# Strassen output block in PSUM: the first product is copied into the second one's bank, and the second accumulates on it

## Chip, cores and metric

The kernel runs on one core of one Trainium2 chip. The metric is the device time of one execution in microseconds (us). It was measured at 535.56 us, the median of 3 runs (535.33 to 535.83).

Engines are named as the profile names them: PE is the matrix engine (PEld its weight loads), DVE the vector engine, ACT the scalar engine, POOL GpSimd, SP the engine whose queue issues the DMAs.

## The reference

A gated linear attention recurrence (4 batches, 8 heads, 768 steps, head size 48) gives 3072 tokens of 384 features. A two-layer network with a hard-swish in the middle follows. Cut to what matters here:

```python
# attention: state = alpha[t] * state + k[t] v[t]^T;  y[t] = q[t] @ state
x = attn_out.transpose(0, 2, 1, 3).reshape(B * S, H * D)   # (3072, 384)
h = x @ w_in                                               # (3072, 2048)
g = h * np.clip(h + 3.0, 0.0, 6.0) / 6.0
return (g @ w_out).astype(np.float32)                      # (3072, 384)
```

Everything is fp32. The change lies in the last product, `g @ w_out`.

## The kernel before

**Tiling.** Tokens are worked off in 24 chunks of 128 (index j) for the attention and in 12 groups of 256 (index g, two chunks) for the network. While the network of group g runs, the attention of later chunks runs between its steps. For groups 2 to 11 the first layer is a fast matrix product of 20 block products (`product1`); for groups 1 to 11 the second layer is a Strassen-like product of 7 block products (`product`). Groups 0 and 1 have other first layers, and group 0 has a plain second one.

**Order.** Nothing reorders the work: `run` (from line 751) walks through a long string of words such as `P.5.0.0` under a manual schedule, and each word issues the instructions of one step. Each engine runs its own instructions in the order of the words; semaphores hold an instruction until what it reads is written and what it overwrites has been read. An instruction that waits holds everything behind it on its engine.

**The words** that this document speaks of (g is the group):

- `M.g.i[.m]`, PE, line 600: block product i of layer 1, four matmuls 128x128x128 into a whole PSUM bank of 512 columns. With m it opens bank m (there are four, `bank_m[0..3]`, line 470), without m it goes on accumulating in the bank of product i-1.
- `n.g.i.z`, ACT, line 606: copies the bank's running sum after product i to SBUF. The next product of the same bank overwrites that sum, so it waits for `n`.
- `o.g.o.step`, DVE, line 610: adds kept sums; with the last step it reads a PSUM bank, and that frees it. `e.g.o`, ACT, lines 619 and 494, and `h.g.o`, DVE, lines 623 and 498: the hard-swish of output block o. Blocks 0 and 1 make the quarter a11 of the hidden tile, 2 and 3 make a12, 4 and 5 a21, 6 and 7 a22.
- `s.g.i`, DVE, line 658: sums of quarters for layer 2.
- `P.g.i[.m]`, PE, line 685: product i of layer 2, eight matmuls into the first 192 columns of a bank, each recorded as two passes (16 records). Products 0, 2, 4 and 6 accumulate one after the other in one bank (`x_t`), 3 and 5 in a second one (`y_t`), and product 1, which is a12 times a block of the weights, has a bank of its own (`z_t`). Product 1's first four matmuls need `h.g.2`, its last four `h.g.3`.
- `K.g.i`, ACT, lines 706 and 680: keeps a running sum in SBUF: K.g.0 the sum after product 0 (tile `p1`), K.g.1 the one after product 2 (`u2`), K.g.2 the one after product 3 (`p5`). Product 2 overwrites what K.g.0 reads, product 4 overwrites what K.g.1 reads, and so they wait for these copies.
- `G.g.i.z`, line 713: the output blocks into the SBUF tile `ohs[z]`. G.g.0 is product 1 (PSUM) plus `p1` (SBUF), one addition on DVE (line 719), and so are G.g.1 and G.g.2 with other sums; G.g.3 is a copy on ACT (line 716). `O.g.i` stores the block through SP's queue (line 724).
- `xc` (sums of x on DVE), `tk`, `ca`, `q`, `qa`, `sc`, `u`, `ya`, `yb`, `cy`, `sv`: steps of the attention and of the inputs that stand between.

The output block of words `K.g.0` and `G.g.0` before:

```python
name, after = [("p1", 0), ("u2", 2), ("p5", 3)][i]        # K: nc.scalar.copy PSUM -> SBUF
kept(g, name, at_t[g, after])
...
after, other = [(1, "p1"), (4, "p5"), (5, "u2")][i]       # G.g.0, G.g.1, G.g.2
nc.vector.tensor_tensor(out=o, in0=at_t[g, after], in1=part_t.pop((g, other)), op=ALU.add)
```

Of the kernel before, what the change touches and what calls it, by code (L numbers as in the profile page):

```python
# [17 lines left out]
def kernel(  # L18
# [32 lines left out]
    nc = tc.nc  # L51
# [633 lines left out]
    def product(g, i, m=None):  # L685
# [6 lines left out]
            (lambda: whole(a12), b[1, 0], z_t, True, True),  # L692
# [13 lines left out]
    def keep2(g, i):  # L706
        name, after = [("p1", 0), ("u2", 2), ("p5", 3)][i]
        kept(g, name, at_t[g, after])
# [4 lines left out]
    def output2(g, i, z):  # L713
        o = oh_t[g, i] = ohs[z]
        if i == 3:
            nc.scalar.copy(out=o, in_=at_t[g, 6])
        else:
            after, other = [(1, "p1"), (4, "p5"), (5, "u2")][i]
            nc.vector.tensor_tensor(out=o, in0=at_t[g, after], in1=part_t.pop((g, other)), op=ALU.add)
# [30 lines left out]
    with tc.manual_schedule():  # L750
# [3 lines left out]
               dx.0 w.2 d2.2 kb.1.0 ck.1 lq.1 r.2 sm.0.1 st.1 tq.1.2 q.1 d3.2 z.0.3 d1.2 dx.2 lv.1.1  # L754
               u.1.3.1 sv.1.0 sm.1.0 p.2 sm.1.1 sc.1.0.2 m.1 ya.0.3 yb.0 cy.0 lq.2 w.1 d1.1 tq.2.1
               q.2 d4.2 lk.2 tk.2.3 k.2 fa.2.0 d4.0 st.2 sc.2.0.2 d2.1 d3.1 m.2 dx.1 d4.1 qa.1.1
               lk.3 la.3 ta.3.1 ca.3 la.4 fa.0.1 sv.1.1 w.3 r.3 ta.4.3 ca.4 r.4 tk.3.1 k.3 kb.2.0
               qa.1.0 d2.3 ya.1.2 yb.1 cy.1 fa.1.2 lq.3 ck.2 d1.3 p.3 d3.3 lv.2.2 u.2.3.2 sm.2.0
               d4.3 fb.2 tq.3.1 q.3 fb.1 qa.2.0 sm.2.1 sv.2.0 st.3 fr.0.2.0 fg.0.2 lk.4 tk.4.0
               sv.2.1 w.5 d2.5 k.4 d3.5 d1.5 qa.3.0 d4.5 qa.2.1 sc.3.1.3 m.3 w.6 d2.6 d1.6 d3.6 d4.6  # L760
               lv.3.0 lq.4 w.7 kb.3.2 fb.0 f.0.3.3 kb.4.0 ya.2.1 ck.3 u.3.3.2 sm.3.0 fr.0.3.1 fg.0.3
               fr.0.1.0 fg.0.1 qa.3.1 sv.3.0 sm.3.1 p.4 d2.7 sv.3.1 d1.7 d3.7 d4.7 f.0.5.0 fr.0.5.1
               fr.0.0.0 fg.0.5 fg.0.0 tq.4.3 ck.4 la.5 ta.5.2 f.0.6.3 ca.5 w.4 d2.4 ya.3.0 yb.3 cy.3
               fr.0.6.1 yb.2 cy.2 w.9 d2.9 q.4 qa.4.1 d1.4 d1.9 dx.4 la.6 w.8 d3.4 r.5 lk.5 w.10
               d3.9 p.5 ca.6 fg.0.6 d4.9 w.12 lq.5 lv.4.1 d2.8 d3.8 f.0.7.2 d1.8 st.4 d4.8 d4.4 w.11
               fr.0.7.0 fg.0.7 f.1.7.0 fr.1.7.1 fg.1.7 sc.4.0.2 m.4 f.1.1.1 fr.1.1.0 fg.1.1 f.1.3.3
               fr.1.3.1 d2.10 d1.10 tk.5.3 f.1.0.2 d2.12 d3.10 d4.10 w.13 fg.1.3 fr.1.0.0 fg.1.0 k.5
               d3.12 lq.6 f.1.6.0 f.1.2.1 u.4.1.0 sm.4.0 d1.12 d4.12 sv.4.0 qa.4.0 ya.4.2 fr.1.6.1
               fg.1.6 w.15 tq.5.3 fa.4.3 sv.4.1 d2.11 kb.5.1 d2.13 fr.1.2.0 f.1.4.2 fr.1.4.1 d1.11
               sm.4.1 q.5 r.6 d3.11 d3.13 fg.1.4 d4.11 lv.5.0 lk.6 tq.6 p.6 d2.15 d3.15 fg.1.2 d1.13  # L770
               d4.13 sc.5.0.3 yb.4 f.1.5.0 fr.1.5.1 fg.1.5 tk.6 m.5 b.1.0.2 fb.4 b.1.1 d1.15 d4.15
               st.5 y.5 w.14 la.7 lk.7 cy.4 d2.14 qa.5.1 ck.5 b.0.0.1 fr.0.4.0 d3.14 k.6 q.6 ca.7
               fg.0.4 d1.14 d4.14 x.0 y.1 y.10 b.0.1 y.0 y.2 u.5.2 P.1.0.0 K.1.0 qa.5.0 sv.5.0
               qa.6.1 P.1.1.3 b.0.2 b.1.2 kb.6.0 ya.5.3 y.6 s.1.0.0 sm.5.0 sv.5.1 G.1.0.0 tk.7
               s.1.1.1 s.1.2.3 x.1 yb.5 cy.5 b.1.3 sc.6.1.2 lv.6.2 ck.6 u.6.3.0 s.1.3.2 x.2 P.1.2
               b.0.3 K.1.1 y.7 s.1.4 s.1.5 y.11 y.3 r.7 xc.2.1 x.3 y.4 y.8 xc.2.3 k.7 xc.2.0 xc.2.4
               y.9 y.12 y.16 y.13 y.15 P.1.3.3 K.1.2 P.1.4 bo.1 P.1.5 xc.2.5 G.1.1.1 P.1.6 y.14 y.17
               y.19 xc.2.6 sm.6.0 G.1.2.2 y.20 M.2.0.2 lv.12.1 la.8 O.1.1 O.1.0 ca.8 y.18 y.21 y.23
               so.1 G.1.3.3 n.2.0.8 bo.0 lq.7 lv.7.0 O.1.2 m.6 xc.2.2 xc.2.10 xc.2.7 tq.7 r.8 p.7
               xc.2.8 sv.6.1 M.2.15.3 M.2.1 kb.7.3 n.2.1.9 M.2.16 M.2.2 n.2.2.10 M.2.7.0 n.2.7.11  # L780
               sm.6.1 xc.2.9 q.7 p.8 M.2.3 M.2.4 n.2.4.12 M.2.8 o.2.0.0 M.2.5 n.2.5.13 qa.7.0 sv.6.0
               st.7 lk.8 O.1.3 lq.8 lk.9 la.9 la.10 tk.8 tq.8 lq.10 lq.9 ya.6.1 yb.6 M.2.9 z.1.3
               M.2.18.1 o.2.1.0 e.2.1.1 M.2.10 cy.6 ck.7 sc.7.0.2 u.7.1.3 n.2.10.14 M.2.11 qa.7.1
               ca.9 la.11 y.22 M.2.6.2 h.2.1 q.8 m.7 e.2.0.0 h.2.0 n.2.11.15 qa.6.0 n.2.18.10 qa.8.1
               M.2.12 M.2.19 n.2.12.12 M.2.13 sm.7.0 sv.7.1 r.9 k.8 o.2.3.0 sv.7.0 ya.7.0 y.24
               o.2.5.0 n.2.13.12 o.2.2.0 yb.7 cy.7 sc.8.1.2 xc.3.1 o.2.2.1 e.2.2.1 xc.3.3 o.2.3.1
               M.2.14 xc.3.4 xc.3.0 xc.3.5 o.2.4.0 xc.3.7 xc.3.6 o.2.6.0 P.2.0.1 M.3.0.2 M.2.17
               h.2.2 o.2.6.1 e.2.3.0 h.2.3 o.2.7.0 K.2.0 n.3.0.12 M.3.1 n.3.1.9 e.2.5.1 M.3.7.0
               n.3.7.13 xc.3.8 o.2.7.1 xc.3.2 kt.8 e.2.6.0 h.2.6 tk.9 M.3.2 n.3.2.10 e.2.4.0 P.2.1.3
               h.2.4 h.2.5 s.2.0.14 e.2.7.0 G.2.0.1 h.2.7 M.3.3 M.3.4 n.3.4.8 k.9 s.2.1.11 M.3.8  # L790
               o.3.0.0 ca.10 kt.9 P.2.3.3 s.2.2.15 s.2.3.14 lv.8.2 kw.8 kr.8 lk.10 sm.7.1 xc.3.9
               M.3.5 n.3.5.11 K.2.2 e.3.0.1 xc.3.10 M.3.9 o.3.1.0 P.2.2 K.2.1 u.8.0.3 M.3.18.2 s.2.5
               M.3.10 n.3.10.14 n.3.18.15 e.3.1.0 s.2.4 P.2.4 tq.9 h.3.0 st.8 sv.8.0 M.3.11 n.3.11.8
               tk.10 p.9 sm.8.0 q.9 r.10 k.10 qa.9.0 qa.9.1 m.8 sm.8.1 h.3.1 M.3.19 o.3.5.0 kt.10
               P.2.5 G.2.2.0 st.9 M.3.12 sc.9.0.1 qa.8.0 n.3.12.10 o.3.3.0 kw.9 lv.9.0 kr.9 sv.8.1
# [4 lines left out]
               xc.4.8 M.4.7.3 M.4.1 xc.4.2 h.3.2 o.3.7.1 lk.11 O.2.2 tk.11 e.3.6.0 e.3.3.1 h.3.3  # L800
               P.3.1.2 e.3.7.1 n.4.1.13 M.4.2 K.3.0 ca.11 q.10 h.3.6 r.11 k.11 h.3.7 n.4.7.15
               lv.10.2 lv.11.0 kw.10 sc.10.0.1 kr.10 G.3.0.0 u.10.3.2 sm.10.0 qa.10.1 n.4.2.14 M.4.3
               M.4.4 M.4.8 s.3.0.9 xc.4.9 s.3.2.12 s.3.1.11 P.3.3.2 n.4.4.8 M.4.5 o.4.0.0 e.4.0.0
               sv.10.1 sm.10.1 xc.4.10 kt.11 O.2.0 O.2.3 lq.11 m.10 s.3.3.9 s.3.5 M.4.9 o.4.1.0
               P.3.2 sv.10.0 st.11 n.4.5.11 K.3.2 la.13 M.4.18.0 p.11 tq.11 lk.12 tk.12 K.3.1 M.4.10
# [3 lines left out]
               k.12 o.4.3.0 m.11 sm.11.0 sv.11.1 kt.12 M.4.13 n.4.13.14 q.12 o.4.3.1 e.4.3.0 o.4.2.0  # L809
               o.4.6.0 h.4.3 o.4.2.1 ya.10.1 ya.11.0 yb.10 yb.11 cy.11 cy.10 xc.5.1 ca.13 xc.5.3  # L810
               M.4.15.1 M.4.16 M.4.14 P.4.0.2 o.4.4.0 M.4.17 xc.5.4 o.4.5.0 xc.5.0 xc.5.5 M.5.0.0
               o.4.6.1 e.4.2.1 h.4.2 P.4.1.3 qa.12.1 e.4.4.0 xc.5.6 o.4.7.0 h.4.4 o.4.7.1 tk.13
               K.4.0 n.5.0.14 M.5.1 e.4.7.1 h.4.7 e.4.5.0 xc.5.2 h.4.5 xc.5.7 G.4.0.3 e.4.6.1 h.4.6
               s.4.1.12 s.4.0.11 xc.5.8 r.13 xc.5.9 xc.5.10 k.13 kw.12 kr.12 la.14 sc.12.2.3
               u.12.0.1 sm.12.0 n.5.1.13 M.5.2 n.5.2.15 M.5.7.1 n.5.7.8 P.4.3.3 s.4.2.9 kt.13 lk.14
               lq.13 O.3.0 O.3.3 lv.13.2 kw.13 O.4.0 lq.14 tq.13 lq.15 M.5.3 M.5.4 M.5.8 s.4.3.10
               P.4.2 sv.12.1 n.5.4.11 o.5.0.0 e.5.0.0 K.4.2 s.4.5 p.13 ca.14 M.5.9 M.5.5 n.5.5.12
               m.12 sm.12.1 o.5.1.0 q.13 P.4.5 K.4.1 G.4.2.0 qa.12.0 qa.18.0 s.4.4 h.5.0 M.5.18.0
               n.5.18.9 o.5.6.0 tk.14 qa.13.0 M.5.10 n.5.10.10 M.5.15.3 M.5.16 M.5.11 M.5.19 r.14
               k.14 n.5.11.11 o.5.7.0 kr.13 u.13.0.2 sc.13.1.3 M.5.12 P.4.4 e.5.1.1 n.5.12.9 M.5.13  # L820
               h.5.1 o.5.4.0 m.13 o.5.5.0 st.13 sv.13.0 ya.13.1 qa.13.1 e.5.4.0 n.5.13.15 sm.13.0
               sv.13.1 h.5.4 la.15 ca.15 sv.12.0 ya.12.3 yb.12 cy.12 yb.13 cy.13 kt.14 G.4.1.2 tq.14
               M.5.14 o.5.6.1 M.5.6.0 xc.6.1 o.5.3.0 xc.6.3 o.5.2.0 xc.6.4 o.5.2.1 e.5.2.1 xc.6.5
               xc.6.0 o.5.3.1 P.4.6 G.4.3.3 xc.6.7 M.5.17 h.5.2 p.14 M.6.0.1 M.6.7.2 e.5.3.0 xc.6.6
               O.3.2 o.5.7.1 q.14 e.5.6.1 n.6.7.8 h.5.6 h.5.3 lk.15 tk.15 n.6.0.9 P.5.0.0 K.5.0
               s.5.0.15 sm.13.1 xc.6.2 r.15 k.15 e.5.7.1 h.5.7 xc.6.8 e.5.5.0 p.15 h.5.5 M.6.1
# [106 lines left out]
```

## Time and profile before

| what | value |
|---|---|
| median of 3 runs | 535.56 us (535.33 to 535.83) |
| span of the profiled execution, first to last instruction | 533.7 us |
| PE busy, matmuls | 524.6 us, 98% |
| DVE busy | 477.2 us, 89% |
| ACT busy | 257.2 us, 48% |
| granted PE clock | 1.000 |
| chain that ended last | PE 85%, DVE 8% |

The profiled execution's span is 1.9 us shorter than the median of the runs, which also count what lies before the first and after the last instruction. In a row of a timeline the columns are start (us from the span's start), duration or extent (us), engine, source line, operation, tiles out<-in, shapes, count, and in brackets the idle time of the engine before the row with what ended it. A row that holds several instructions is merged.

### The profile page before, as it was taken

Reading aid. Unit: us, or ns where it says so; the run is one execution under the profiler, and the core shown is the slowest. Engines: PE = TensorE matmul, PEld = TensorE weight load, DVE = VectorE, ACT = ScalarE, POOL = GpSimd, SP = SyncE. Lnnn points to the kernel's source line nnn. Section 1 sums busy time; section 2 is a strip of 40 time slices with the busy share of each in tenths; the row PEclk is TensorE's granted clock in tenths of the full one; section 3 lists DMA queues with packets and bytes.
Section 4 is the critical chain, followed back from the end, with each engine's and each line's share of the span. In section 5 each row is a group of like instructions: output and inputs, shape, how many; then the busy total and the mean of one; then the engine's idle time right before and its main releaser. Section 6 shows DMA issues by size and latency. Waiting matters only on the chain.

```text
span 533.7 us, 15143 instructions
## 1 busy us (share of the span) xinstructions
PE 524.6 (98%) x6306; PEld 499.4 (94%) x6306; DVE 477.2 (89%) x849; ACT 257.2 (48%) x503; POOL 50.4 (9%) x71
## 2 busy tenths in 40 slices
PE   8799999999999999999999999999999999999997
PEld 7698886789999999999999999999999999999997
DVE  6999989999999999998999999999999899496382
ACT  3889865212653553553544444642634544553340
POOL 5333425100000000000000000000000000000000
DMA  9998876005615155254344355044454042100001
GB/s 174 217 252 256 215 216 152 21 2 154 152 30 116 32 121 135 57 140 95 87 110 113 91 124 140 19 120 102 115 136 104 11 110 43 44 2 2 15 16 37
DMA packets 124100, 54.40 MB, mean 102 GB/s; under 512 B 83328, under 2 KB 116864, under 8 KB 124032
## 3 DMA queue, kind: packets, MB, share of 16 engines
q1 hardware_dynamic: 124032, 53.44, 42.5%
q8 instruction: 49, 0.80, 0.6%
q14 instruction: 19, 0.16, 0.1%
HBM read 44.50 MB, written 8.91 MB: 100 GB/s over the span
## 4 chain that ended last, share of the span: by engine, by line
PE 85%; DVE 8%; POOL 2%; DMA 2%; ACT 1%; issue 1%; SPq 1%; DVEq 0%; POOLq 0%
PE m_ps L703 34%; PE m_ps L600 34%; PE m_ps L478 5%; PE t_ps L455 4%; PE t_ps L346 2%; PE t_ps L429 2%; PE m_ps L489 2%; PE t_ps L282 1%; DVE rings L647 1%; DMA v<-in_v_dram 1%; DVE raw L537 1%; ACT raw L191 1%; DMA kq<-in_k_dram 1%; DVE g_sb L647 1%; DVE w L537 1%
## 5 line engine op out<-in xcount | busy, mean ns | idle before, releaser
L606 ACT COPY g_sb<-m_ps 128x512 f32<-128x512 f32 x110 | 63.6, 584 | 124.9 <-PE m_ps L600 104.1
L703 PE MATMUL m_ps<-w,g_sb 128*128 128x192 f32 x704 | 121.7, 327 | 0.0
L703 PEld LDWEIGHTS m_ps<-w,g_sb 128*128 128x128 f32 x704 | 113.7, 190 | 0.4
L703 PE MATMUL m_ps<-rings,g_sb 128*128 128x192 f32 x528 | 91.5, 326 | 0.0
L703 PEld LDWEIGHTS m_ps<-rings,g_sb 128*128 128x128 f32 x528 | 85.4, 190 | 0.1
L600 PE MATMUL m_ps<-xc,w 128*128 128x128 f32 x640 | 82.7, 277 | 0.3 <-DVE w L541 0.3
L600 PEld LDWEIGHTS m_ps<-xc,w 128*128 128x128 f32 x640 | 77.5, 192 | 1.5 <-issue 0.5
L494 ACT ACTIVATE r<-g_sb,half 128x512 f32<-128x512 f32 x80 | 56.8, 722 | 32.9 <-DVE g_sb L541 12.1
L498 DVE SCALAR_TENSOR_TENSOR g_sb<-r,g_sb 128x512 f32<-128x512 f32 x80 | 53.6, 682 | 4.6 <-ACT r L494 4.2
L600 PE MATMUL m_ps<-xT,raw 128*128 128x128 f32 x400 | 52.5, 277 | 0.0
L600 PEld LDWEIGHTS m_ps<-xT,raw 128*128 128x128 f32 x400 | 48.6, 192 | 0.6
L409 POOL TENSOR_TENSOR st<-sm,R 128x192 f32<-128x192 f32 x20 | 12.9, 643 | 353.8 <-DVE sm L439 306.7
L647 DVE TENSOR_TENSOR g_sb<-g_sb 128x512 f32<-128x512 f32 (+1 forms) x55 | 42.0, 795 | 0.2
L600 PE MATMUL m_ps<-xT,w 128*128 128x128 f32 x320 | 42.0, 276 | 0.0
L600 PEld LDWEIGHTS m_ps<-xT,w 128*128 128x128 f32 x320 | 39.3, 192 | 0.1
L366 ACT COPY A<-q 48x256 f32<-48x256 f32 x88 | 35.5, 404 | 5.0 <-DVE q L332 3.7
L356 DVE TENSOR_TENSOR A<-t_ps,mask 64x256 f32<-64x256 f32 x96 | 36.0, 414 | 0.4
L478 PE MATMUL m_ps<-xT,w 128*128 128x256 f32 x144 | 32.8, 382 | 0.0
L600 PE MATMUL m_ps<-xc,raw 128*128 128x128 f32 x240 | 31.8, 276 | 0.0
L309 DVE TENSOR_TENSOR_SCAN R<-t,ones 128x516 f32<-128x516 f32 x24 | 29.7, 1236 | 1.1 <-ACT t L300 1.0
L478 PEld LDWEIGHTS m_ps<-xT,w 128*128 128x128 f32 x144 | 26.7, 190 | 3.6
L600 PEld LDWEIGHTS m_ps<-xc,raw 128*128 128x128 f32 x240 | 29.6, 192 | 0.1
(104 smaller groups left out, 731.0 us busy)
## 6 DMA issues: line engine op xcount, KB each, us to landing
raw<-in_moe_w_out_dram SPq DMA_DIRECT2D x8, 768.0 KB, 5.2
raw<-in_moe_w_in_dram SPq DMA_DIRECT2D x6, 768.0 KB, 6.8
v<-in_v_dram SPq DMA_DIRECT2D x48, 96.0 KB, 3.0
out_dram<-oh SPq DMA_DIRECT2D x44, 96.0 KB, 1.7
far<-kq SPq DMA_DIRECT2D x64, 64.0 KB, 2.2
kb<-far SPq DMA_DIRECT2D x64, 64.0 KB, 2.0
aq<-in_alpha_dram SPq DMA_DIRECT2D x36, 96.0 KB, 2.5
qq<-in_q_dram SPq DMA_DIRECT2D x36, 96.0 KB, 2.4
```

Of the source, the lines that this page charges most:

```text
L309: nc.vector.tensor_tensor_scan(out=reverse(R, n - 1, n), data0=reverse(ax, n, n), data1=reverse(ones, n, n), initial=0.0, op0=ALU.mult, op ...
L356: nc.vector.tensor_tensor(out=to[:, a], in0=sc[a][half], in1=mask[half, half].unsqueeze(1).to_broadcast([HB, NP, HB]), op=ALU.mult)
L366: nc.scalar.copy(out=to[:, a], in_=Q_t[j][64 * a : 64 * a + D, :, half])
L409: nc.gpsimd.tensor_tensor(out=st, in0=sm, in1=R_t[j][:, :, 0:1].to_broadcast([C, NP, D]), op=ALU.mult)
L455: nc.tensor.matmul(y_of(j, (i + 1) // 2, p)[:, HB * b : HB * b + HB], vb[:, p, e : e + 32], A_t[j][:, b, 2 * p + a], start=(b == 0 and i = ...
L478: nc.tensor.matmul(h[:, f], w1[:, kk, o : o + C], xT_t[g][:, kk], start=(kk == 0), stop=(kk == KT - 1))
L494: nc.scalar.activation(out=to, in_=h, func=AF.Relu, bias=half, scale=1.0 / 6.0)
L498: nc.vector.scalar_tensor_tensor(out=to, in0=r, scalar=1.0, in1=h, op0=ALU.min, op1=ALU.mult)
L600: nc.tensor.matmul(acc[g][i][:, f * C : (f + 1) * C], spots[w][:, f * C : (f + 1) * C], x_of(g, x), start=(first and f == 0), stop=last, s ...
L606: nc.scalar.copy(out=slots[z], in_=acc[g][i])
L647: nc.vector.tensor_tensor(out=out, in0=in0, in1=in1, op=ALU.subtract)
L703: nc.tensor.matmul(to[g], a, rhs[:, f], start=(first and f == 0), stop=(last and f == HF - 1), skip_group_check=True)
```

## The change

For groups 2 to 11, K.g.0 no longer copies product 0's sum to SBUF but to the first 192 columns of the bank in which product 1 will run, that is from PSUM to PSUM, on ACT. Product 1's first matmul no longer starts a new sum (`start` is false) and so accumulates on the copy. The bank then holds the whole output block (0, 0), and G.g.0 becomes a plain copy from PSUM to `oh` on ACT, where it was an addition on DVE. Group 1 stays as it was.

```diff
-            (lambda: whole(a12), b[1, 0], z_t, True, True),
+            (lambda: whole(a12), b[1, 0], z_t, m is not None, True),
...
-    def keep2(g, i):
+    def keep2(g, i, m=None):
+        if m is not None:
+            z_t[g] = bank_m[m][:, 0:HD]
+            nc.scalar.copy(out=z_t[g], in_=at_t[g, 0])
+            return
         name, after = [("p1", 0), ("u2", 2), ("p5", 3)][i]
         kept(g, name, at_t[g, after])
...
-        if i == 3:
-            nc.scalar.copy(out=o, in_=at_t[g, 6])
+        if i == 3 or i == 0 and (g, "p1") not in part_t:
+            nc.scalar.copy(out=o, in_=at_t[g, 6 if i else 1])
```

In the string of words the bank number moves from `P.g.1.m` to `K.g.0.m` (the banks are the same). K.g.0 is moved in five groups: from behind P.g.1 to ahead of it in groups 3, 4, 7 and 8, and to a later place ahead of it in group 2. In the other five it keeps its place, which is ahead of P.g.1 already. All other words keep their order. The words around each place after the change:

```text
g=2  n.3.1.9 e.2.5.1 ... n.3.7.13 xc.3.8 o.2.7.1 K.2.0.3 xc.3.2 kt.8 e.2.6.0 ... M.3.2 ... P.2.1     (K was ahead of n.3.0.12 M.3.1)
g=3  h.3.2 o.3.7.1 K.3.0.2 lk.11 O.2.2 tk.11 e.3.6.0 e.3.3.1 h.3.3 P.3.1 e.3.7.1 n.4.1.13 M.4.2      (K was after M.4.2)
g=4  M.5.0.0 o.4.6.1 K.4.0.3 e.4.2.1 h.4.2 P.4.1 qa.12.1 e.4.4.0 ... n.5.0.14 M.5.1                  (K was after tk.13, ahead of n.5.0.14)
g=5  P.5.0.0 K.5.0.3 ... e.5.7.1 ... e.5.5.0 ... h.5.5 M.6.1 P.5.1 G.5.0.1 n.6.1.13 M.6.2            (not moved)
g=6  P.6.0.1 K.6.0.0 M.7.1 P.6.1                                                                    (not moved)
g=7  G.6.3.1 o.7.7.1 K.7.0.2 h.7.2 ... e.7.6.1 n.8.1.12 ... M.8.2 n.8.2.9 P.7.1                      (K was after e.7.4.1 h.7.4)
g=8  n.9.1.9 P.8.0.1 K.8.0.3 ... e.8.3.1 ... M.9.2 P.8.1                                            (K was after n.9.7.13)
g=9  n.10.2.14 h.9.4 h.9.5 K.9.0.3 e.9.7.1 ... P.9.1                                                (not moved)
g=10 e.10.6.1 K.10.0.3 e.10.4.0 P.10.1                                                              (not moved)
g=11 P.11.3.2 K.11.0.0 ... P.11.2 ... K.11.2 ... P.11.1 G.11.0.2 s.11.5 O.11.0 K.11.1 P.11.4 G.11.1.0 P.11.5   (not moved)
```

G.g.0 stands at the same words as before in all groups; only its engine is another.

## The prediction

> **What bounds the kernel now.** I read the busy times of the engines first, then the same by stretches of the span, then what the weight loads of PE waited for, then the durations of the operations that the change touches, and last the timeline of each of the ten places.
>
> ```profile
> span 533.7 us, 15143 instructions
> PE 524.6 (98%) x6306; PEld 499.4 (94%) x6306; DVE 477.2 (89%) x849; ACT 257.2 (48%) x503; POOL 50.4 (9%) x71
> ```
>
> PE leads, DVE is second and ACT has half its time free. An average says nothing of the stage that is changed, so the stretches follow (columns: stretch, its length, busy time and count of PE, PEld, DVE, ACT, POOL, the granted clock, DMA share, GB/s), and after them all that PE's weight loads waited for from 130 us on.
>
> ```profile
> 130.00:200.00 70.00, 70.00 (x954) 68.39 (x956) 67.89 (x126) 36.94 (x76) 2.92 (x4) 1.00 0.41 95
> 200.00:300.00 100.00, 100.00 (x1221) 98.79 (x1214) 95.41 (x175) 45.12 (x94) 3.54 (x5) 1.00 0.45 106
> ...
> 400.00:500.00 100.00, 100.00 (x1174) 98.66 (x1174) 79.03 (x147) 45.12 (x93) 1.54 (x3) 1.00 0.18 43
> ```
>
> ```profile
> PEld t_ps L429 <- issue: 0.5, 2, 0.2
> PEld t_ps L346 <- issue: 0.5, 2, 0.2
> ```
>
> All ten changed places lie between 149 and 524 us. In that stretch PE is busy without a gap, at full clock, and neither DVE nor ACT ever holds it: the two rows left are its own issue. So time taken off DVE or ACT gains nothing there, and every wait that reaches PE is added to the end, since PE has no idle time in which to catch up.
>
> **The durations.** Columns: busy total, mean ns of one, idle before.
>
> ```profile
> L719 DVE TENSOR_TENSOR oh<-m_ps,p 128x192 f32<-128x192 f32 x22 | 7.7, 349 | 8.7 <-PE m_ps L703 8.5
> L682 ACT COPY p<-m_ps 128x192 f32<-128x192 f32 x22 | 7.0, 318 | 24.1 <-PE m_ps L703 24.1
> L716 ACT COPY oh<-m_ps 128x192 f32<-128x192 f32 x11 | 3.5, 315 | 25.2 <-PE m_ps L703 25.2
> ```
>
> Per group the change takes one addition of 349 ns from DVE, keeps one copy on ACT with another destination, and adds one copy of 315 ns to ACT: over ten groups 3.5 us less on DVE, 3.2 us more on ACT. Neither number is on the path. PE's work is the same: product 1 was eight matmuls and is eight matmuls, and products whose first matmul doesn't start a sum (product 2, also L703) take the same 0.163 us from record to record. No DMA is added or moved; the stores wait for G as before, and the `oh` buffer that each G.g.0 takes had its last store issued at least 7 us earlier (group 6: 315.3 against 322.7; the median store lands 1.7 us after issue).
>
> A copy from PSUM to PSUM isn't in the trace. The nearest rows are L682 (318 ns) and the two forms of L494 at 128x512, 684 ns from PSUM and 722 ns from SBUF: 38 ns between the memories on the reading side. I take 0.32 us, with 0.28 and 0.36 as ends. The Trainium skill, "ScalarE: Activation LUTs", in the section "Step-by-step: what each stage is for", has it that ScalarE reaches PSUM faster than SBUF; by that rule the lower end would hold, and one place below, group 2, would be 0.04 us cheaper, which doesn't alter the forecast. No row here shows the writing side.
>
> **The new waits.** Two things are new. P.g.1's first weight load waits for K.g.0 (the waits of L703 sit on weight loads), and K.g.0 waits for its bank, so for the last reader of it on DVE; and G.g.0 now waits for the end of P.g.1 at the head of ACT's queue, where it stood in DVE's. Behind K and G stand ACT instructions that PE or DVE need. Steps from one engine to the next, by the trace: PE's end to ACT's start 0.04 us (276.69 to 276.73), DVE's end to ACT's start 0.03 (h.3.2's end at 194.45 to e.3.3.1's start at 194.48), ACT's end to a weight load 0.06 (16.80 to 16.86, early in the run where PE waited for ACT), DVE's end to a weight load 0.05 (22.06 to 22.11). After a 128x192 copy ACT starts the next one 0.21 us later (K at 276.73, the next at 276.94 in the fence below), after a 128x512 copy 0.47 and after a 128x512 activation 0.62.
>
> Group 5, where G stands ahead of n.6.1.13, which M.6.2 needs. First ACT's, then PE's weight loads' timeline:
>
> ```profile
> 276.73 0.32 ACT L682 COPY p<-m_ps 128x192 f32<-128x192 f32 x1 [1.53 <-PE m_ps L703]
> 276.94 1.33 ACT L494 ACTIVATE r<-g_sb,half 128x512 f32<-128x512 f32 x2
> 278.18 0.57 ACT L606 COPY g_sb<-m_ps 128x512 f32<-128x512 f32 x1
> ...
> 277.31 2.58 PEld L703 LDWEIGHTS m_ps<-w,g_sb 128*128 128x128 f32 x16
> 279.86 1.02 PEld L600 LDWEIGHTS m_ps<-xT,raw 128*128 128x128 f32 x8
> ```
>
> n.6.1.13 ran at 278.18, during P.5.1 (loads from 277.31, last matmul's end 280.18). Now G.5.0.1 is ahead of it and waits for that end: G at 280.22, n at 280.43, its end at 281.00, and the load of M.6.2, due at 279.86, at 281.06 to 281.08. **Cost 1.21 us**, a full round PE, ACT, ACT, PE, which nothing covers, because M.6.2 is the very next step of PE.
>
> Group 11, where G stands ahead of K.11.1, which P.11.4 needs:
>
> ```profile
> 520.46 0.32 ACT L682 COPY u<-m_ps 128x192 f32<-128x192 f32 x1 [1.05 <-PE m_ps L703]
> ...
> 520.10 2.63 PEld L703 LDWEIGHTS m_ps<-w,g_sb 128*128 128x128 f32 x16
> 522.70 2.63 PEld L703 LDWEIGHTS m_ps<-rings,g_sb 128*128 128x128 f32 x16
> ```
>
> K.11.1 ran at 520.46, while P.11.1 computed. Now G.11.0.2 waits ahead of it for P.11.1's end at 523.02: G 523.06, K.11.1 523.27 to 523.59, and P.11.4's load, due at 522.70, at 523.65. **Cost 0.95 us.** P.11.5 and P.11.6 follow without slack, so it moves the end.
>
> Group 2, K itself late: o.2.7.1 frees bank 3 at 155.93, and K stands behind n.3.7.13, which starts at 155.84. So K starts at 155.84 + 0.47 = 156.31 and ends at 156.63; P.2.1's load, due at 156.26, comes at 156.69. **Cost 0.43 us** (0.39 to 0.47 by the ends of the copy).
>
> Group 4, K as a stopper: it waits for P.4.0's end at 233.26 and runs 233.30 to 233.62, ahead of e.4.2.1, which ran at 229.10. Now e.4.2.1 runs 233.51 to 234.23, h.4.2 (DVE, 0.70) 234.27 to 234.97, and P.4.1's load, due at 234.78, comes at 235.02. Cost 0.24, taken as **0.22 us**, since PE is late by group 2's wait already while parts of this chain start from DVE; ends 0 and 0.45 (DVE is 1.5 us behind afterwards, and n.5.1.13 comes out at 239.67 against M.5.2's load at 239.55 plus the lateness, so a second 0.2 can follow).
>
> Group 3, the same with more cover: K waits for o.3.7.1 (end 195.04) and runs 195.07 to 195.39; e.3.6.0 195.28, e.3.3.1 195.90 to 196.62, h.3.3 196.66 to 197.33. Its reader, the fifth matmul of P.3.1, loads at 197.08, so 0.30 late, or not at all if PE comes 0.43 later. I take **0.15 us**, ends 0 and 0.30.
>
> Group 9: K ran at 443.03 to 443.35 and P.9.1's load at 443.00, so 0.41 as it stands. But K was late only because e.9.5.0 waited for DVE (441.94); with PE 2 us late by then, DVE and K come earlier relative to it. The floor is n.10.2.14 after M.10.2's end at 442.00: K 442.51, end 442.83, no wait. I take **0.10 us**, ends 0 and 0.41.
>
> The other four cost nothing, because K ends before the load of P.g.1 is due: group 6 316.94 + 0.06 against 317.20, group 7 358.02 (K after o.7.7.1's end at 357.66) against 361.02, group 8 400.38 against 401.92, group 10 481.12 against 481.56. Group 5's K too (277.05 + 0.06 against 277.31). The cover is the steps of `M` between products 0 and 1; in groups 5 and 6 only 0.20 us of it is left, so a copy 0.2 us dearer would show there. The other G.g.0 have ACT steps behind them that PE wants later, and P.g.3, which takes the same bank after G.g.0, loads 1.1 us after it or more.
>
> **Sum.** 0.43 + 0.15 + 0.22 + 1.21 + 0.10 + 0.95 = 3.06 us. Span 533.7 + 3.06 = 536.8; median 535.56 + 3.06 = **538.6 us**. With all low ends 0.39 + 0 + 0 + 1.17 + 0 + 0.91 = 2.5; with all high ends 0.47 + 0.30 + 0.45 + 1.25 + 0.41 + 0.99 = 3.9, and if each of ten K and P takes one more semaphore instruction (51 ns in L703's rows) 4.9. The likeliest case's own range is 538.0 to 540.5.
>
> **Rivals.**
>
> First, faster: DVE's relief wins. It lies at 200 to 400 us, where DVE is 95% busy. Freed of 3.5 us, it would give 532.1 if PE were held by DVE throughout and no copy came late. It decides if DVE's holds on PE there exceed 3.06 us; the waits show 0.0, so I give it 3%.
>
> Second, no change: the lateness is made up. ACT is half idle, and if M.6.2 and P.11.4 found their banks free in time the rest (0.90 us) would lie within 0.2%, about 536.4. Against it: the order of words on ACT is fixed, and G can't start before the product that it copies has ended. 7%.
>
> Third, much slower: lateness spreads. Group 4 leaves DVE 1.5 us behind in a stretch where it has 5% to spare, so more sums (s.4.0 for P.4.3, `xc` for M.5.7) could come late, as could the hard-swish in groups 3 and 7. Another wait of group 4's size in each of five groups (5 x 0.4) gives 540.6 and more. For it: DVE's 95%. Against it: DVE gets back 0.35 us per group, and s.4.0 comes out some 0.1 us ahead of its load. 12%.
>
> That the change doesn't do what it says, because the matmul overwrites the copy, would leave these times as they are. The Trainium skill, "PSUM — Partial Sum Buffer", section "The four PSUM rules", says that a write of ScalarE doesn't mark an element as written, and that a later matmul adds only where an earlier matmul has left the mark; no row of a trace can show that.
>
> **Numbers.** The forecast has 78%, the three rivals 3, 7 and 12%. Range 537.3 to 540.6: its low end takes in a case in which one of the two large waits is 1.2 us cheaper, its high end the start of the third rival. 0.2% (1.07 us) is about what a measurement of this kernel can tell from no change. Faster by more 3%, within 7%, slower by more 90%.
>
> **What would show it.** In the profile after, PE's weight loads of L600 wait for ACT `g_sb` L606 about 1.2 us near 282 us, and those of L703 wait for ACT L682 about 0.9 us near 526 us and 0.4 us near 157 us; DVE's busy time falls by 3.5 us and ACT's rises by 3.2; the row of the new copy is 0.28 to 0.36 us; PE's other steps keep their length. I would be wrong if PE shows no wait for ACT at 280 us, or many small waits in the groups that I costed at nothing.

## The result: slower by 0.7%, and the profile after

The changed kernel takes 539.26 us (median of 4 runs, 538.85 to 540.06) against 535.69 us of the kernel before on the same chip (535.33 to 535.85). The ratio is 1.0068 with a 95% interval of 1.0054 to 1.0083, so 3.6 us more (2.9 to 4.4). The forecast was 538.6 us, 3.06 us more, with a range of 537.3 to 540.6.

The page of the profile after, its span and busy times:

```profile
span 538.1 us, 15166 instructions
PE 526.3 (98%) x6306; PEld 499.7 (93%) x6306; DVE 475.3 (88%) x839; ACT 259.6 (48%) x513; POOL 50.4 (9%) x71
```

The averages hide the loss: PE still reads 98%. DVE lost its ten additions and ACT gained ten copies. What PE's weight loads waited for from 130 us on tells it (columns: who, for whom, us in total, times, longest):

```profile
PEld m_ps L600 <- ACT g_sb L606: 1.2, 1, 1.2
PEld m_ps L703 <- ACT u L682: 0.9, 1, 0.9
PEld m_ps L703 <- ACT m_ps L709: 0.8, 2, 0.5
PEld m_ps L703 <- DVE g_sb L498: 0.5, 2, 0.3
PEld t_ps L429 <- issue: 0.5, 2, 0.2
PEld t_ps L346 <- issue: 0.5, 2, 0.2
```

The last two rows were there before. The first four are new and hold six waits; a seventh, of 0.07 us, is too small for a row. The operations that the change touches, with their new line numbers (709 is the copy into the bank, 720 the copy into `oh`, 723 the addition):

```profile
L709 ACT COPY m_ps<-m_ps 128x192 f32<-128x192 f32 x10 | 3.1, 308 | 14.4 <-PE m_ps L703 10.8 <-DVE g_sb L539 3.6
L720 ACT COPY oh<-m_ps 128x192 f32<-128x192 f32 x21 | 6.6, 316 | 32.8 <-PE m_ps L703 32.7
L723 DVE TENSOR_TENSOR oh<-m_ps,p 128x192 f32<-128x192 f32 x12 | 4.1, 345 | 7.3 <-PE m_ps L703 7.2
```

The copies cost what such copies cost (315 to 318 ns before); none of this is the loss.

To see where PE falls back, I took the start of every weight load in both traces, load by load, and the difference between them. It is a step function: flat, with a jump wherever PE waits for something new.

| where (time in the kernel before) | first late load | forecast, us | measured jump, us |
|---|---|---|---|
| group 2, 156.26 | P.2.1, waits for K.2.0 | 0.43 | 0.43 |
| group 3, 197.08 | P.3.1, fifth matmul, waits for h.3.3 | 0.15 | 0.38 |
| group 4, 234.78 | P.4.1, waits for h.4.2 | 0.22 | 0.24 |
| group 4, 239.55 | M.5.2, waits for n.5.1.13 | named as possible | 0.07 |
| group 5, 279.86 | M.6.2, waits for n.6.1.13 | 1.21 | 1.22 |
| group 9, 443.00 | P.9.1, waits for K.9.0 | 0.10 | 0.42 |
| group 11, 522.70 | P.11.4, waits for K.11.1 | 0.95 | 0.95 |

After three of them 0.05 us is given back at the next load, and a few hundredths drift between. From 0.90 us at 129 us of the span the difference grows to 4.40 us at the last load, 3.50 us through the changed stretch, which is the measured 3.6 us. The 0.90 us come from the start of that one execution, before the first changed word; in the other traces below it is 0.05 to 1.10 us.

Group 5 in the profile after, ACT and then PE's weight loads:

```profile
278.65 0.30 ACT L709 COPY m_ps<-m_ps 128x192 f32<-128x192 f32 x1 [1.53 <-PE m_ps L703]
278.87 1.33 ACT L494 ACTIVATE r<-g_sb,half 128x512 f32<-128x512 f32 x2
282.14 0.32 ACT L720 COPY oh<-m_ps 128x192 f32<-128x192 f32 x1 [1.94 <-PE m_ps L703]
282.36 0.59 ACT L606 COPY g_sb<-m_ps 128x512 f32<-128x512 f32 x1
...
283.00 0.97 PEld L600 LDWEIGHTS m_ps<-xT,raw 128*128 128x128 f32 x8 [1.19 <-ACT g_sb L606]
```

Read it from the bottom: the load of M.6.2 sits 1.19 us until L606 (n.6.1.13) has ended; L606 starts behind L720 (G.5.0.1); and L720 had ACT idle for 1.94 us, waiting for product 1 to end. Before the change the same L606 ran right behind the L494 pair, during product 1. In group 11 it is the same with L682 (K.11.1) behind L720:

```profile
526.57 0.32 ACT L720 COPY oh<-m_ps 128x192 f32<-128x192 f32 x1 [3.65 <-PE m_ps L703]
526.78 0.32 ACT L682 COPY u<-m_ps 128x192 f32<-128x192 f32 x1
...
527.16 1.92 PEld L703 LDWEIGHTS m_ps<-rings,g_sb 128*128 128x128 f32 x12 [0.93 <-ACT u L682]
```

### The profile page after: what moved, and what is told of

The parts are those of the page before. It is cut to its first block, busy times and chain, and to the rows that moved or that the text cites. A ratio compares the mean times of both kernels' runs of the same rounds, so it can differ in the third digit from the quotient of the medians.

```text
span 538.1 us, 15166 instructions
## 1 busy us (share of the span) xinstructions
PE 526.3 (98%) x6306; PEld 499.7 (93%) x6306; DVE 475.3 (88%) x839; ACT 259.6 (48%) x513; POOL 50.4 (9%) x71
## 4 chain that ended last, share of the span: by engine, by line
PE 83%; DVE 10%; DMA 3%; ACT 1%; issue 1%; SPq 0%; POOL 0%; DVEq 0%; ACTq 0%; POOLq 0%
PE m_ps L703 32%; PE m_ps L600 32%; PE m_ps L478 6%; PE t_ps L455 4%; PE t_ps L346 2%; PE t_ps L429 2%; DMA v<-in_v_dram 2%; PE m_ps L532 1%; PE m_ps L489 1%; PE m_ps L516 1%; DVE rings L647 1%; DVE R L309 1%; DVE raw L537 1%; DVE g_sb L647 1%; DVE w L537 1%
## 5 line engine op out<-in xcount | busy, mean ns | idle before, releaser
L606 ACT COPY g_sb<-m_ps 128x512 f32<-128x512 f32 x110 | 63.5, 584 | 114.7 <-PE m_ps L600 98.2
L494 ACT ACTIVATE r<-g_sb,half 128x512 f32<-128x512 f32 x80 | 56.7, 722 | 29.4 <-DVE g_sb L541 11.7
```

The costliest lines, as they stand in the source:

```text
L494: nc.scalar.activation(out=to, in_=h, func=AF.Relu, bias=half, scale=1.0 / 6.0)
L606: nc.scalar.copy(out=slots[z], in_=acc[g][i])
```

## Experiments

The theory is called "order": the loss is the place of K.g.0 and G.g.0 in ACT's queue and whom they hold from there, not the price of the copy or of the accumulation. Its first rival, "copy", has the copy between banks or the accumulation on it cost something in every group. The second question is the size of groups 3 and 9, where the forecast gave a discount for PE being late already.

**G moved back on ACT.** The changed kernel, with two words (and one store) moved:

```diff
-h.5.5 M.6.1 P.5.1 G.5.0.1 n.6.1.13 M.6.2
+h.5.5 M.6.1 P.5.1 n.6.1.13 G.5.0.1 M.6.2
...
-P.11.1 G.11.0.2 s.11.5 O.11.0 K.11.1 P.11.4
+P.11.1 s.11.5 K.11.1 G.11.0.2 O.11.0 P.11.4
```

> The changed kernel with G.5.0 behind n.6.1.13 and G.11.0 behind K.11.1 on ACT, nothing else. Theory 'order' (G at the head of ACT's queue holds n.6.1.13 and K.11.1): the two waits of PE of 1.2 us near 282 us and 0.95 us near 527 us go, the others (0.43, 0.33, 0.24, 0.07, 0.42) stay: 539.26 - 2.1 = 537.1 us. Rival 'copy' (the PSUM to PSUM copy, or the accumulation on it, costs the time in every group, about 0.35 us each): nothing changes, 539.3 us.

Measured: 537.61 us, ratio 1.0038 (1.0023 to 1.0053). The jumps at 279.86 and 522.70 are gone, the other five stand at 0.43, 0.38, 0.24, 0.08 and 0.42 us, 1.5 us through the stretch. The median is 0.5 us above the expected one, though the steps are as expected and the spans of the two traces differ by 2.2 us (538.1 and 535.9). What makes the rest isn't settled; the start of the program alone differs by such amounts from one execution to the next (this trace is 0.7 us late at 129 us, see the last section). ACT's timeline of this kernel, near 282 us:

```profile
279.99 0.57 ACT L606 COPY g_sb<-m_ps 128x512 f32<-128x512 f32 x1
282.03 0.32 ACT L720 COPY oh<-m_ps 128x192 f32<-128x192 f32 x1 [1.47 <-PE m_ps L703]
```

The copy into `oh` waits for PE as before, but n.6.1.13 has run ahead of it and nobody waits behind it.

**G on DVE.** The changed kernel with the plain copy on the engine that had the addition:

```diff
-        if i == 3 or i == 0 and (g, "p1") not in part_t:
-            nc.scalar.copy(out=o, in_=at_t[g, 6 if i else 1])
+        if i == 3:
+            nc.scalar.copy(out=o, in_=at_t[g, 6])
+        elif i == 0 and (g, "p1") not in part_t:
+            nc.vector.tensor_copy(out=o, in_=at_t[g, 1])
```

> The changed kernel with G.g.0 as a plain copy on DVE, in the place it had before; K.g.0 and the accumulation stay. 'order': as with G moved back, the two large waits go and 537.1 us are left, since DVE reads G where it always did. 'copy': 539.3 us, since copy and accumulation are still there. If DVE's load were what holds PE, this would be slower than 537.1.

Measured: 537.46 us, ratio 1.0031 (1.0021 to 1.0042), 1.5 us through the stretch, with the same five jumps and 0.05 us at 241.33 besides. DVE is back at 477.4 us of busy time, and that doesn't show in the total: moving G back on ACT and moving it to DVE are worth the same.

**G on ACT alone.** The kernel before, with only `i == 3 or i == 0 and g > 1` as the condition of the copy on ACT; K.g.0 goes to SBUF as before. This kernel leaves product 0's sum out of its output block, so it shows times alone.

> The kernel before with G.g.0 of groups 2 to 11 as a copy on ACT; product 0's sum still goes to SBUF and is left out of output block (0, 0). 'order': waits of 1.2 us near 280 us and 0.95 us near 523 us and no other, +2.1 us. 'copy': no wait at all, +0.

Measured: 537.77 us in one run, 2.05 us through the stretch, in two jumps: 1.22 us at 279.86 and 0.95 us at 522.70. What its weight loads wait for, but for their own issue:

```profile
PEld m_ps L600 <- ACT g_sb L606: 1.2, 1, 1.2
PEld m_ps L703 <- ACT u L682: 0.9, 1, 0.9
```

The two large waits need neither the copy between banks nor the accumulation. They belong to G's place alone.

**K's place alone.** The kernel before, with the words K.g.0 where the change has them, the copy still to SBUF and P.g.1 opening its bank:

```diff
-h.2.3 o.2.7.0 K.2.0 n.3.0.12 M.3.1
+n.3.7.13 xc.3.8 o.2.7.1 K.2.0 xc.3.2
...
-o.4.7.1 tk.13 K.4.0 n.5.0.14
+M.5.0.0 o.4.6.1 K.4.0 e.4.2.1 h.4.2 P.4.1.3
```

(groups 3, 7 and 8 in the same way.)

> The kernel before with K.g.0 alone moved to where the change has it; it still copies to SBUF, and P.g.1 doesn't wait for it. 'order': only group 4's wait is left (K waits for P.4.0 ahead of e.4.2.1), 0.24 us near 235 us and perhaps 0.07 near 240, since in groups 2, 3 and 9 the copy doesn't wait for its bank or P.g.1 not for the copy; +0.3 us. If 0.4 us show in groups 2 or 9 too, the wait there isn't that for the copy.

Measured: 536.14 us in one run. Group 4 shows 0.24 and 0.07 us, with 0.05 at 241.33 besides, and groups 2, 3 and 9 show nothing where they did. One jump wasn't expected: 0.19 us at 162.79, in the fifth matmul of P.2.3.

```profile
PEld m_ps L703 <- DVE g_sb L664: 0.2, 1, 0.2
PEld m_ps L703 <- DVE g_sb L498: 0.2, 1, 0.2
```

The first row is that one: L664 is s.2.1, which DVE reaches later because K.2.0 now stands ahead of e.2.6.0, on which DVE waits. In the changed kernel it doesn't show; there PE is 0.43 us late by then and DVE has one addition less. "G on DVE" tells the two apart: its copy on DVE takes 349 ns, as the addition did, and still s.2.1 ends at 163.54 and the load that needs it starts at 163.77 without a wait. So PE's lateness is enough to hide it.

The run also bounds what the place alone does. The waits of groups 2, 3 and 9, together 1.23 us of the 3.50, need the new destination as well: only when K writes the bank does it wait for the bank's last reader (group 3), and only then does PE's load wait for K (groups 2 and 9).

**The change with other places.** All of it is kept; only words on ACT move, besides the two of the first experiment:

```diff
-n.3.7.13 xc.3.8 o.2.7.1 K.2.0.3 xc.3.2
+xc.3.8 o.2.7.1 K.2.0.3 n.3.7.13 xc.3.2
...
-o.3.7.1 K.3.0.2 lk.11 O.2.2 tk.11 e.3.6.0 e.3.3.1 h.3.3 P.3.1
+o.3.7.1 lk.11 O.2.2 tk.11 e.3.6.0 e.3.3.1 K.3.0.2 h.3.3 P.3.1
...
-o.4.6.1 K.4.0.3 e.4.2.1 h.4.2 P.4.1 qa.12.1 e.4.4.0
+o.4.6.1 e.4.2.1 qa.12.1 e.4.4.0 K.4.0.3 h.4.2 P.4.1
...
-e.9.5.0 k.23 xc.10.8
+K.9.0.3 e.9.5.0 k.23 xc.10.8
```

> The change kept whole, with other places of ACT's words: G.5.0 behind n.6.1.13, G.11.0 behind K.11.1, and K.g.0 behind the ACT steps that don't wait for its product (group 3 behind e.3.3.1, group 4 behind e.4.4.0) or ahead of those that it needn't follow (group 2 ahead of n.3.7.13, group 9 ahead of e.9.5.0). 'order': 0.08 us is left near 156 us (bank 3 is free at 155.93, copy 0.32, load due at 156.26), nothing else: within 0.2% of the kernel before, 535.7 us. DVE's 3.5 us of relief bring nothing, since PE waits for DVE nowhere. 'copy': 538 us or more.

Measured: 536.28 us (11 runs) against 535.71 us (15 runs), ratio 1.0012 (1.0003 to 1.0021). In the trace a single jump of 0.06 us is left, at 156.26. The spans of these runs have a median of 534.0 us against 533.9 us of the kernel before; of the 0.6 us between the medians some 0.3 lies outside the span (2.1 us against 1.8), and what makes it isn't settled. So the copy between banks and the accumulation cost PE nothing in ten groups, and DVE's relief (474.8 us of busy time against 477.2) makes it no faster than the kernel before. It may cover one wait: in group 2 s.2.1 ends at 162.86 and the load that needs it starts at 162.91, so an addition more on DVE (0.26 us from start to start at 160.56 in the kernel before) would, by estimate, have made that load late by as much. No version here beats the kernel before.

**Each copy twice.**

```diff
-            nc.scalar.copy(out=z_t[g], in_=at_t[g, 0])
+            for _ in range(2):
+                nc.scalar.copy(out=z_t[g], in_=at_t[g, 0])
```

> The changed kernel with each copy K.g.0 made twice, 0.21 us more on ACT in each of ten groups. 'order' (only where the copy stands on the chain does it count): groups 2, 3, 4 and 9 each wait 0.21 longer, so 0.64, 0.54, 0.45 and 0.63 us; groups 5 and 6, which had 0.20 us left, 0 to 0.05; groups 7, 8, 10 and 11 nothing; the waits for G (1.2 and 0.95) as before. Together 4.3 to 4.4 us after the start where the changed kernel had 3.5. 'copy': 10 x 0.21 = 2.1 more.

Measured: 541.78 us in one run, 5.15 us through the stretch. The places were right and the price of a copy wrong. Groups 2, 3, 4 and 9 jump by 0.77, 0.72, 0.58 and 0.76, each 0.34 more; groups 5 and 6 show 0.11 and 0.17 at the load of P.g.1; groups 7, 8 and 10 show nothing, and the waits for G stand at 1.22 and 0.95. ACT's timeline shows why 0.34 and not 0.21:

```profile
156.99 0.67 ACT L710 COPY m_ps<-m_ps 128x192 f32<-128x192 f32 x2
157.57 0.73 ACT L494 ACTIVATE r<-g_sb,half 128x512 f32<-128x512 f32 x1
```

The two copies take 0.67 us: the second starts 0.03 us after the first has ended, while the L494 behind them starts 0.09 us before the second ends. In the trace each second copy waits for the semaphore that ACT's own instructions raise: the program holds it until the first is written. Groups 5 and 6 confirm the margin of 0.20 us that the prediction read off: 0.34 - 0.20 is 0.14, between their 0.11 and 0.17.

**PE made late far ahead, and close by.** Both have four idle matmuls at two places. Far: ahead of sc.9 and sc.20. Near: ahead of M.4.7.3 and sc.22.

```diff
+    def idle_t(i, n):
+        for _ in range(n):
+            nc.tensor.matmul(banks[i][:, 0:C], ident, ident, start=True, stop=True)
...
-M.3.12 sc.9.0.1        la.22 sc.20.0.2
+M.3.12 zt.0.4 sc.9.0.1 la.22 zt.0.4 sc.20.0.2
```

> The changed kernel with four idle matmuls (0.9 us of PE) ahead of sc.9, near 180 us, and of sc.20, near 400 us: PE is made late long before the waits of groups 3 and 9, with a place in between where DVE waits for PE (188.5 and 427.6 us in the changed kernel). Theory 'inherited' (DVE and ACT wait for PE in between and take the lateness over): the waits near 198 and 446 us stay at 0.33 and 0.42. Rival 'cover' (the prediction's discount: a late PE meets them in time): both gone.

> The changed kernel with four idle matmuls ahead of M.4.7.3 (near 195 us) and of sc.22 (near 445 us), that is behind the last place where DVE waits for PE and ahead of P.3.1 and P.9.1. 'inherited': DVE and ACT don't take this lateness over, and both waits are gone; in their place stand 2 x 0.9 us of idle matmuls. 'cover' says the same here. If the waits stay, K's chain hangs on PE more closely than the timeline shows.

Measured: far, the idle matmuls add 0.89 us each time and the jumps at 197.08 and 443.00 stay, 0.38 and 0.40 us. Near, they add 0.94 and 0.89 us, and both jumps are gone. The waits of "near", but for issue and the two of G, one each of groups 2 and 4:

```profile
PEld m_ps L708 <- ACT m_ps L714: 0.4, 1, 0.4
PEld m_ps L708 <- DVE g_sb L498: 0.2, 1, 0.2
```

(Lines are five further down, for the added helper.) In the kernel before, DVE's timeline has the places where it takes PE's lateness over, ahead of groups 3 and 9:

```profile
187.21 0.29 DVE L537 TENSOR_TENSOR xc<-xT 128x128 f32<-128x128 f32 x1 [1.19 <-ACT xT L464]
```

```profile
424.49 0.36 DVE L719 TENSOR_TENSOR oh<-m_ps,p 128x192 f32<-128x192 f32 x1 [1.43 <-PE m_ps L703]
427.87 0.36 DVE L439 TENSOR_TENSOR s<-t_ps,st 128x192 f32<-128x192 f32 x1 [0.65 <-PE t_ps L429]
```

At 187.21 DVE waits 1.19 us for ACT's copy of the attention's output, which itself waits for PE (0.57 us); at 424.49 and 427.87 it waits for PE directly. The same three in the changed kernel:

```profile
188.50 0.29 DVE L537 TENSOR_TENSOR xc<-xT 128x128 f32<-128x128 f32 x1 [1.15 <-ACT xT L464]
```

```profile
427.58 0.36 DVE L723 TENSOR_TENSOR oh<-m_ps,p 128x192 f32<-128x192 f32 x1 [1.50 <-PE m_ps L703]
430.95 0.36 DVE L439 TENSOR_TENSOR s<-t_ps,st 128x192 f32<-128x192 f32 x1 [0.65 <-PE t_ps L429]
```

They start 1.29, 3.09 and 3.08 us later, and PE's weight loads there are 1.29 and 3.09 us late: DVE has taken over the whole lateness. What follows on DVE and ACT is then as late as PE, and covers nothing.

## Why the prediction was right, and where it was off

Direction and mechanism were right: a PE without a gap, nothing to gain on DVE, and every new wait added to the end. Point by point:

- The two large waits, both for G.g.0 at the head of ACT's queue, came out at 1.22 and 0.95 us against 1.21 and 0.95. "G moved back", "G on DVE" and "G on ACT alone" take them away or leave only them.
- Group 2 was right to the hundredth (0.43) and group 4 within 0.02 (the 0.24 worked out, before 0.02 was taken off for earlier lateness, is what came); the second wait of group 4, given as possible, is 0.07 us. The four groups costed at nothing cost nothing, and group 5's own copy too.
- Mis-sized were groups 3 and 9. The prediction worked out 0.30 and 0.41 us "as it stands" and then took 0.15 and 0.10, with the reason that PE is late by then and K's chain comes earlier relative to it. Measured are 0.38 (0.05 of it given back at the next load) and 0.42. The step that failed is that discount: DVE waits for PE between the earlier waits and these places, so both are equally late. "Far" and "near" show it: lateness from ahead of such a place changes nothing, lateness from behind it hides the wait whole. Without the discount the sum would have been 0.43 + 0.30 + 0.24 + 1.21 + 0.41 + 0.95 = 3.54 us, against 3.50 in the trace.
- The copy from PSUM to PSUM takes 308 ns on average (median 303), inside the 280 to 360 that were given. The rule of the Trainium skill, "ScalarE: Activation LUTs", "Step-by-step: what each stage is for", that PSUM is the faster destination, agrees in sign: 308 against 319 for the same copy to SBUF (L682 into `p`, same profile). That is 11 ns, where the prediction's low end allowed for 38.
- The busy times moved as forecast in sign only: DVE's fell by 1.9 us and ACT's rose by 2.4, not by 3.5 and 3.2. The forecast added up whole records, but neighbours overlap (the copy at 278.65 takes 0.30 us and the next instruction starts at 278.87), and busy time counts an overlap once; whether that is the whole difference isn't settled.
- Of the rivals, DVE's relief made no kernel faster than the one before, as its 0.0 of PE's waits had said, and the lateness of group 4 didn't spread beyond 0.07 us. That the lateness is made up later is excluded by the flat stretches between the jumps.

## What to carry to other kernels

Where the leading engine has no gap, don't count busy time that is moved between the others; list the instructions that stand behind each moved one in its new queue, and ask whom each of them holds. A short instruction that waits for the leading engine's latest result belongs behind everything that this engine needs next: here two words moved were worth 2.0 us in the trace, and a few more the other 1.4. When several waits are added up, a later one is discounted for earlier lateness only if its chain doesn't wait for the late engine in between.

## What was not expected of the hardware

Two copies on ACT that write the same place in PSUM follow each other at 0.34 us, where two 128x192 copies to different tiles in SBUF start 0.21 us apart (526.57 and 526.78 in the profile after). The second of the pair carries a wait for ACT's own semaphore; whether the engine would hold it back without that isn't shown.

The start of the program, up to 35 us, differs between executions by as much as 1.1 us in the traces taken here. In four of them ("G moved back", "G on DVE", "far" and "near") the granted clock was 0.5 for 3.4 us between 22 and 27 us, which makes 0.89 on average from 20 to 35 us, and they are 0.54 to 1.10 us late at 129 us. The clock isn't all of it: the changed kernel's trace has 1.00 there and is 0.90 us late. So a difference of a few tenths is read from the steps in the trace, not from two spans.
